# A two-layer attention and gated-MLP kernel: loads reordered, constants moved off the front of VectorE, tiles normalized one by one, and a planner with traced transfer and fetch times

## The chip, the cores and the metric

The kernel runs on one core of a Trainium2 chip. The metric is the device time of one execution in microseconds (us). Quoted times are medians of several executions.

A core has five engines that run their own instruction streams and wait for one another through semaphores: TensorE (PE, matmuls; its weight loads are PEld), VectorE (DVE), ScalarE (ACT), GpSimd (POOL) and SyncE (SP), which here only starts transfers. ScalarE starts a few transfers too, on a queue of its own.

## The reference

Two rounds of windowed attention and a gated MLP, each with a residual, on one sequence of 2048 rows of 512 elements in bfloat16.

```python
def _A_ref(x, wqkv, wo):                      # 32 heads of 16, window of 256 keys, causal
    q, k, v = split_heads(x @ wqkv)           # (cut: reshape and transpose)
    scores = einsum("bhqd,bhkd->bhqk", q, k) * Dh ** -0.5
    p = softmax(where(mask, scores, -1e9))
    return merge_heads(einsum("bhqk,bhkd->bhqd", p, v)) @ wo

def _B_ref(x, w_gate, w_up, w_down):          # F = 1792
    return (sigmoid(x @ w_gate) * (x @ w_up)) @ w_down

x = A_x
x = x + _A_ref(_layernorm(x), A_wqkv, A_wo)
x = x + _B_ref(_layernorm(x), B_w_gate, B_w_up, B_w_down)
x = x + _A_ref(_layernorm(x), A_wqkv, A_wo)   # the same weights again
x = x + _B_ref(_layernorm(x), B_w_gate, B_w_up, B_w_down)
```

## The kernel before

The rows are 16 tiles of 128, in four groups of four. The program that builds the kernel holds a **planner**: a small model of the engines and transfers that runs while the instructions are written, keeps for each engine a queue of ready tasks with a priority, and emits whatever the model finds free. On the chip each engine then executes its instructions in that fixed order. If the model is wrong about when something is ready, the order is still correct, but an engine stands behind a wait while later work would have been possible.

The assumed times of the kernel before, and the way it models a transfer and an instruction fetch:

```python
EXP_NS = 1880                 # one exponential on ScalarE
EXTRA = {"ACT": 40, "DVE": 10, "POOL": 30, "SP": 70}
COLD = 13600                  # matmuls are taken as twice as long before this time
DMA_LATENCY = 1500            # issue done to landed
FETCH = (1200, 1300)
...
    def land(self, t, since):
        if self.fetched >= since - FETCH[0]:
            self.at(self.fetched + FETCH[0] + FETCH[1], t.done.fire)
        else:
            t.done.fire()
    def dma(self, ns, nbytes, fn, deps=(), prio=5, after=0, queue="SP"):
        def go(e):
            fn()
            self.dma_free = max(self.dma_free, self.now + ns) + nbytes / 250.0
        ...
```

Each tile is normalized in three steps on two engines: its statistics on VectorE, the root (one over the square root of the variance) on GpSimd, and the normalizing itself on VectorE again. `prio` is 0 for the first group and 2 for the others; a lower number goes first, and among equals the one that was ready first.

X of tiles 8 to 11 comes behind the output weights and half of the gate and up weights:

```python
    def loads(...):
        ...                                        # (cut) x of tiles 0 to 3, two tiles at a time, on SP and ACT
        for i, k in enumerate("kqv"):              # three thirds of the qkv weights, on ACT
            self.has_wq[k] = load(self.wq[:, :, h], wq_src[:, :, h], D * D * 2, prio=0, queue="ACT" if i < 3 else "SP")
        x_group(1, 0)                              # x of tiles 4 to 7
        gap, at = 1600, 6000
        self.has_wo = load(self.wot[:], wo_src, D * D * 2, after=at)
        ...                                        # first half of gate and up, then
                x_group(2, at)                     # x of tiles 8 to 11, then the second half, down, x of 12 to 15
```

Small transfers copy v, shifted by half a tile, two tiles at a time, to Vl and Vh, for the edges of the window.

```python
        self.Vaug = [big.tile([P, NBG, VW], BF16, name=f"Vaug{i}") for i in range(3)]
        ...
            dst = self.Vaug[gi % 3][:, t % NBG, 0:VS * H]...       # the copy of tile t out of PSUM
        ...
                to, of = dst[e * HP:e * HP + HP, :, e * n:e * n + n], V[z:P:2, o:o + 2, e * n:e * n + n]
                parts.append(pl.dma(580, HP * n * 4, lambda to=to, of=of: nc.sync.dma_start(out=to, in_=of), deps, 3).done)
```

Where the model sees PE without work, it emits four dummy matmuls, so that the granted clock stays up:

```python
    def keep_warm(self, bank):
        for i in range(4):
            nc.tensor.matmul(self.banks[bank][:, 0:P], lhsT=self.ident[:], rhs=self.ident[:], start=True, stop=True)
        pl.count(4)
        pl.matmul("d", 4 * 56)
```

The softmax here doesn't subtract the row's maximum and nothing guards it: scores larger than these inputs give would overflow.

## Time and profile before

| kernel before | value |
|---|---|
| time, median of 3 (lowest to highest) | 552.1 us (551.35 to 553.03) |
| span of the profiled run | 551.2 us, granted clock 0.997 |
| PE busy, next engine | 96%, VectorE 75% |
| dummy matmuls in the order | 88 (56 of them first) |

The prediction below shows the page's shares, PE's waits, the opening and two stretches of the clock. A row of the timeline is: start, duration, engine, line, operation, result <- inputs, sizes, count; in brackets, how long the engine stood idle before it and what released it.

Two rows of the timeline of the kernel before matter later and aren't in the prediction. They show when the second group of tiles (4 to 7) got going:

```profile
23.71 0.41 DVE L520 TENSOR_SCALAR xn<-xsb,st 128x512 bf16<-128x512 bf16 x1
...
26.31 0.81 PE L572 MATMUL bank<-xnT,wq 128*128 128x512 bf16 x2
```

Its last tile, 7, is normalized at 23.71, and PE starts q of the group (512 columns at a time) at 26.31, without a wait in front of it.

### The profile page before, as it was taken

The numbers are of one execution on the slowest core, as the hardware profiler recorded it, in microseconds if no ns is written. First come the engines' busy times: TensorE is split into PE (matmuls) and PEld (weight loads), VectorE is DVE, ScalarE is ACT, GpSimd is POOL, SyncE is SP. The second block draws the span as 40 slices with busy tenths as digits, with TensorE's granted clock in tenths as the row PEclk, the third lists the DMA queues.
The fourth block names the chain that finished last, engine by engine and source line by source line (L and its number), as shares of the span: only waits on it lengthen the run. The fifth ranks groups of instructions, "written<-read, shape, count | busy, mean of one in ns | idle before, by whom it ended". The sixth has DMA issues, their size and how long they took to land.

```text
span 551.2 us, 24123 instructions
## 1 busy us (share of the span) xinstructions
PE 527.5 (96%) x10851; PEld 354.7 (64%) x10944; DVE 414.5 (75%) x906; ACT 395.5 (72%) x459; POOL 63.1 (11%) x145
## 2 busy tenths in 40 slices
PE   7998999999999999989999999999999999999996
PEld 6546857756657656656566765666656666767874
DVE  6997889788799799679677696868767677756432
ACT  3897878888888887657587877868788776742321
POOL 5221110110011120002110021000100000000000
PEclk8999999999999999999999999999999999999999
DMA  8694412322334332214401143022541332122000
GB/s 276 209 170 147 51 39 56 65 44 63 46 52 75 64 40 58 45 32 98 70 6 37 42 89 62 12 51 61 96 62 23 40 81 60 41 50 59 21 21 29
DMA packets 97015, 36.41 MB, mean 66 GB/s; under 512 B 79248, under 2 KB 96912, under 8 KB 96912
## 3 DMA queue, kind: packets, MB, share of 16 engines
q1 hardware_dynamic: 95040, 33.04, 30.1%
q8 instruction: 85, 1.39, 1.1%
q10 hardware_dynamic: 1872, 1.84, 1.1%
q14 instruction: 18, 0.15, 0.1%
HBM read 9.70 MB, written 2.10 MB: 21 GB/s over the span
## 4 chain that ended last, share of the span: by engine, by line
PE 87%; DVE 4%; DMA 4%; issue 3%; ACT 1%; POOL 0%; DVEq 0%; ACTq 0%
PE bank L662 33%; PE bank L695 16%; PE bank L932 8%; PE Sps L853 7%; PE bank L723 5%; PE bank L572 5%; PE bank L637 5%; PE bank L601 5%; PE Sps L863 2%; DMA xnT<-xn 2%; DMA OnT<-On 1%; ACT PTring L905 1%; DVE st L498 1%; PE bank L532 1%; DMA out_dram<-xsb 1%
## 5 line engine op out<-in xcount | busy, mean ns | idle before, releaser
L905 ACT ACTIVATE PTring<-Sps 128x2048 bf16<-128x2048 f32 (+1 forms) x122 | 225.9, 1851 | 55.2 <-PE Sps L853 52.3
L662 PE MATMUL bank<-xnT,wg 128*128 128x256 bf16 (+1 forms) x1064 | 140.6, 256 | 0.1
L662 PE MATMUL bank<-xnT,wu 128*128 128x256 bf16 (+1 forms) x1064 | 140.5, 256 | 0.0
L674 ACT ACTIVATE th<-bank 128x256 bf16<-128x256 f32 x224 | 80.2, 384 | 47.9 <-PE bank L662 42.4
L677 DVE SCALAR_TENSOR_TENSOR hT<-th,bank 128x256 bf16<-128x256 bf16 x224 | 87.5, 414 | 30.8 <-ACT th L674 29.8
L695 PE MATMUL bank<-wd,hT 128*128 128x512 bf16 x402 | 103.6, 379 | 2.5 <-issue 1.0
L662 PEld LDWEIGHTS <-wg 128*128 128x128 bf16 x1064 | 88.5, 98 | 23.5 <-issue 1.7
L662 PEld LDWEIGHTS <-wu 128*128 128x128 bf16 x1064 | 90.9, 98 | 12.3 <-issue 0.9
L503 POOL TENSOR_SCALAR st<-st 128x1 f32<-128x1 f32 x64 | 18.6, 291 | 442.4 <-DVE st L499 442.4
L905 ACT ACTIVATE edge<-Sps 128x2048 bf16<-128x2048 f32 (+1 forms) x32 | 56.7, 1773 | 16.8 <-PE Sps L863 16.1
L791 DVE TENSOR_TENSOR PTring<-PTring,mask 128x1024 bf16<-128x1024 bf16 x64 | 44.0, 687 | 30.8 <-ACT PTring L905 30.7
L695 PEld LDWEIGHTS <-hT 128*128 128x128 bf16 x448 | 41.8, 98 | 37.8 <-issue 0.8
L932 PE MATMUL bank<-PTring,Vaug 128*32 128x64 bf16 (+1 forms) x2880 | 52.1, 203 | 3.6 <-issue 3.5
L932 PEld LDWEIGHTS <-Vaug 128*32 128x32 bf16 x2880 | 44.0, 97 | 13.7 <-issue 10.6
L555 DVE CAST OTs<-bank 128x512 bf16<-128x512 f32 x54 | 39.2, 728 | 15.1 <-PE bank L932 14.7
L853 PE MATMUL Sps<-qT,kTp 32*128 32x64 bf16 (+3 forms) x1856 | 47.8, 218 | 1.4 <-ACT PTring L905 0.3
L853 PEld LDWEIGHTS <-kTp 32*128 32x128 bf16 x1856 | 24.5, 92 | 36.7 <-issue 35.0
L932 PE MATMUL bank<-edge,Vl 128*32 128x64 bf16 x1024 | 44.5, 193 | 0.0
L498 DVE BATCH_NORM_STATS2 st<-xsb 128x6 f32<-128x512 bf16 x64 | 43.7, 683 | 0.4
L791 DVE TENSOR_TENSOR edge<-edge,maske 128x1024 bf16<-128x1024 bf16 x60 | 40.8, 682 | 3.3 <-ACT edge L905 3.2
L504 POOL TENSOR_TENSOR st<-st,nhalf 128x1 f32<-128x1 f32 x64 | 40.9, 640 | 5.3
L932 PE MATMUL bank<-edge,Vh 128*32 128x64 bf16 x896 | 40.8, 193 | 0.0
(72 smaller groups left out, 527.1 us busy)
## 6 DMA issues: line engine op xcount, KB each, us to landing
Vl<-Vaug SPq DMA_DIRECT2D x32, 68.0 KB, 2.2
out_dram<-xsb SPq DMA_DIRECT2D x32, 64.0 KB, 1.9
Vh<-Vaug SPq DMA_DIRECT2D x28, 68.0 KB, 2.3
wg<-in_B_w_gate_dram SPq DMA_DIRECT2D x2, 896.0 KB, 11.6
wu<-in_B_w_up_dram SPq DMA_DIRECT2D x2, 896.0 KB, 9.5
wd<-in_B_w_down_dram SPq DMA_DIRECT2D x7, 256.0 KB, 4.4
wq<-in_A_wqkv_dram ACTq DMA_DIRECT2D x3, 512.0 KB, 8.0
xsb<-in_A_x_dram SPq DMA_DIRECT2D x6, 256.0 KB, 6.4
```

The lines of the kernel that those rows point to most:

```text
L498: nc.vector.bn_stats(out=st[:, 0:6], in_=self.xsb[:, t, :])
L504: nc.gpsimd.tensor_tensor(out=st[:, 8:9], in0=st[:, 9:10], in1=self.nhalf[:], op=ALU.pow)
L555: self.nc.vector.tensor_copy(out=out, in_=in_)
L572: return [(mm_ns(w), lambda kt=kt, o=o: nc.tensor.matmul(self.banks[bank][:, o:o + w], lhsT=self.wq[:, kt, cq * P:cq * P + P], rhs=self.xn ...
L662: return [(mm_ns(w), lambda i=i, j=j, fc=fc, wt=wt, kt=kt: nc.tensor.matmul(pt[:, i, j, :], lhsT=wt[:, kt, fc * P:(fc + 1) * P], rhs=self. ...
L674: nc.scalar.activation(out=box["th"][0][:], in_=pt[:, 0, :], func=AF.Tanh, scale=0.5)
L677: nc.vector.scalar_tensor_tensor(out=self.hT[:, chunk, :], in0=box["th"][0][:], scalar=1.0, in1=pt[:, 1, :], op0=ALU.add, op1=ALU.mult)
L695: nc.tensor.matmul(self.banks[bank][:], lhsT=self.hT[:, c, o:o + P], rhs=self.wd[:, fc, :], start=fc == 0, stop=fc == FC - 1)
L791: done = pl.task({"DVE": dve_bf_ns(1024)}, lambda e: nc.vector.tensor_tensor(out=r, in0=r, in1=m.to_broadcast([P, 16, HP]), op=ALU.mult), ...
L853: nc.tensor.matmul(self.sps[:, m, o:o + n * HP], lhsT=kTp[32 * m:32 * m + 32, i, tt, e, :], rhs=self.qT[32 * m:32 * m + 32, i, q0:q0 + n * ...
L905: nc.scalar.activation(out=out, in_=src, func=AF.Exp, scale=scale)
L932: nc.tensor.matmul(o, lhsT=Va[:, c0:c0 + 32], rhs=p(h), start=k == 0 or t == 0, stop=k == len(parts) - 1 or t == 0, tile_position=(0, 32 * g))
```

## The change

The intent: let VectorE reach x sooner (its memsets go to GpSimd or stay behind, the masks wait), normalize the first tiles one by one so that PE starts sooner, bring all weights in the order in which they are wanted, and let the planner work with times taken from traces: how long a transfer needs to land, when an instruction block is fetched and what that delays. The core of the diff:

```diff
-EXTRA = {"ACT": 40, "DVE": 10, "POOL": 30, "SP": 70}
+EXTRA = {"ACT": 40, "DVE": 10, "POOL": 30, "SP": 0}
-COLD = 13600
+COLD = 5200
-DMA_LATENCY = 1500
-FETCH = (1200, 1300)
+LAND = 1230
+BULK = (240.0, 370.0)
+LANES = 8
+LEAD = (65, 40)
+LINE_NS = 3550
+FETCH = (1200, 2300)
@@ a transfer lands a fixed time after its issue, later if a fetch falls into it, or behind the bulk loads
+    def land(self, t, end):
+        base, nbytes, bulk = t.transfer
+        if bulk:
+            self.dma_free = max(self.dma_free, end + 1500) + nbytes / bulk
+            at = self.dma_free
+        else:
+            at = end + base
+            for f in self.fetches[-3:]:
+                if end < f + FETCH[0] < at - 400:
+                    at = max(at, f + FETCH[1] + (1550 if f + FETCH[0] < end + 500 else 1100))
+            at = max(at, self.dma_free + 300)
@@ loads
-        for i, k in enumerate("kqv"):
-            h = slice("qkv".index(k) * D, ("qkv".index(k) + 1) * D)
-            self.has_wq[k] = load(self.wq[:, :, h], wq_src[:, :, h], D * D * 2, prio=0, queue="ACT" if i < 3 else "SP")
+        self.has_wq["q"] = self.has_wq["k"] = both([
+            load(self.wq[:, k:k + 2, 0:2 * D], wq_src[:, k:k + 2, 0:2 * D], 4 * P * D * 2, prio=0, queue=q)
+            for k, q in ((0, "ACT"), (2, "SP"))])
+        self.has_wq["v"] = load(self.wq[:, :, 2 * D:3 * D], wq_src[:, :, 2 * D:3 * D], D * D * 2, prio=0, queue="ACT")
+        x_group(1)
+        self.has_wo = load(self.wot[:], wo_src, D * D * 2)
+        x_group(2)
+        gu = [load(w[:, k:k + 2, :], src[:, k:k + 2, :], 2 * P * F * 2)
+              for w, src in ((self.wg, wg_src), (self.wu, wu_src)) for k in (0, 2)]
+        self.has_gu = both(gu)
+        at = 26000
+        x_group(3, at)
@@ constants: the memsets of Vl go to GpSimd, as 32-bit words
-            eng = nc.vector if z == 0 else nc.gpsimd
             for V in self.Vd[z]:
-                eng.memset(V[0:HP, :, n:VW], 0.0)
+                for part, a, b in ((slice(0, HP), n, VW), (slice(HP, P), 0, n), (slice(HP, P), 2 * n, VW)):
+                    nc.gpsimd.memset(V[part, :, a:b].bitcast(F32), 0.0)
@@ masks behind the first roots
-        a = pl.task({"POOL": 900}, mask, prio=7, port=True)
+        a = pl.task({"POOL": 900}, mask, [self.roots["p", 0, 0, NBG - 1]], prio=7, port=True)
@@ one by one
-        c = pl.task({"DVE": 406}, apply, [b.done], prio, can, port=True)
+        c = pl.task({"DVE": 406}, apply, [b.done], -1 if key == ("p", 0, 0) else prio, can, port=True)
@@ the transpose after attention
-        b = pl.dma(1800, 262144, turn, [box[0], box[1]], 0 if early else 2)
+        b = pl.dma(1250, 262144, turn, [box[0], box[1]], 0 if early else 2, base=1950)
```

Cut: the model of fetched instruction blocks, the limit of eight transfers in flight, helper functions, and further issue times (1210 to 1240 ns and the like). The arithmetic is unchanged.

## The prediction

> **What bounds the kernel now.** I read the page's shares first, then the list of what TensorE (PE) waited for, then the opening of the timeline, then the table of stretches.
>
> ```profile
> PE 527.5 (96%) x10851; PEld 354.7 (64%) x10944; DVE 414.5 (75%) x906; ACT 395.5 (72%) x459; POOL 63.1 (11%) x145
> ...
> PEclk8999999999999999999999999999999999999999
> ...
> q8 instruction: 85, 1.39, 1.1%
> ```
>
> PE is busy for 96% of the span and no other engine for more than 75%. The page's mean for a gate matmul, 256 ns, is its whole latency and not its share of the time, so I took the start-to-start distances of the matmuls from the trace. A 256-column gate or up matmul follows its neighbour after 109 ns, a 512-column one after 216 ns, nearly everywhere. Setting each kind of neighbour at its median distance and adding up gives 529.7 us of PE work that cannot be squeezed without dropping instructions. The span is then: start 1.44 us, work 529.7, tail after the last matmul starts 4.5, and the rest, about 15.6 us, is waiting and slow clock: PE falls 5.5 us behind those medians in the first 22 us, 2.1 more at 42.8, and 8 more after 60. That rest is all that a reordering can win.
>
> The waits of PE, in us in total, times, longest:
>
> ```profile
> PE bank L932 <- issue: 3.5, 2, 2.3
> PE bank L572 <- DMA xnT<-xn: 3.1, 2, 2.0
> PE bank L532 <- DVE xn L520: 2.0, 1, 2.0
> PE bank L1112 <- POOL ident L438: 1.4, 1, 1.4
> PE bank L723 <- DMA OnT<-On: 1.2, 2, 0.7
> ```
>
> These five make 11.2 us. The first is PE with no instruction to run, the second and fifth are DMA transposes that land late, the third is the first normalized tile. The fourth is the start itself, which the change leaves alone.
>
> The opening (start us, duration us, engine, line, work, count):
>
> ```profile
> 4.83 0.64 DVE L498 BATCH_NORM_STATS2 st<-xsb 128x6 f32<-128x512 bf16 x1
> ...
> 8.00 1.02 DVE L520 TENSOR_SCALAR xn<-xsb,st 128x512 bf16<-128x512 bf16 x3
> ...
> 8.44 1.42 PE L532 MATMUL bank<-ident,xn 128*128 128x128 bf16 x12 [1.96 <-DVE xn L520]
> ...
> 9.67 0.61 PE L601 MATMUL bank<-xnT,wq 128*128 128x128 bf16 x4
> ```
>
> VectorE (DVE) starts the statistics at 4.83 although the first part of x was in at 4.02 (ScalarE's table load is released by it then): memsets were still in front. It then takes all four tiles' statistics before the first is normalized at 8.00. The dummy warm-up matmuls ended at 6.47, so PE idles 1.96 us, and then runs slowly:
>
> ```profile
> 5.00:10.00 5.00, 3.04 (x41) 2.84 (x39) 4.81 (x18) 1.27 (x4) 3.08 (x8) 0.85 1.07 359
> 10.00:15.00 5.00, 4.95 (x69) 3.73 (x69) 2.53 (x8) 3.25 (x7) 0.42 (x2) 0.81 1.09 367
> ```
>
> Third from the end is the granted clock (0.85, 0.81), last the GB/s. Every later stretch up to 500 us has clock 1.00.
>
> **What the Trainium skill says.** "Perfetto Trace Analysis", opening note: matmul busy time is a bad measure of distance to the roofline, because matmuls are pipelined; weight-load share is a better one. The trace agrees: 96% busy beside 64% weight load, and 256 ns of latency beside 109 ns of spacing. "TensorE: Matmul & The Clock Gate", Part 1: PE runs at half clock until a window of about 3.4 us has been busy, and falls back after an idle one; warm spacing is N/2.4 ns + 2.5. The trace agrees (109 and 216 ns warm, 107 ns for 128 columns cold), and the slow stretch follows the idle gap. "Runtime: NRT & Kernel Launch", Instruction fetch mechanics: instructions stream in in blocks of 16 KiB, 256 instructions, "mostly hidden". The trace has 85 such packets (1.39 MB), and 21,890 PE instructions make 85.5 blocks; but the 2.3 us wait on "issue" follows the start of one such packet by 0.4 us, so it isn't always hidden. "DMA: Bandwidth & Descriptors", Specifications: some 358 GB/s of HBM per core; the trace shows 359 to 369 between 5 and 20 us.
>
> **The change part by part.** The kernel carries a planner that fixes the order of instructions from assumed times, so I compared the built order of both programs; arithmetic is the same.
>
> (a) Off the front of DVE: the six memsets of Vl (2 x (0.31 + 0.28 + 0.09) = 1.4 us) go to GpSimd, as 32-bit words. GpSimd's own six drop by about half (0.60, 0.55, 0.15 us now) and it gets twelve, at some 0.3, 0.28 and 0.1 us: 4 x 0.7 = 2.7 us, estimated from those rows, and its two masks (0.9 us) move behind the first roots. It stays free before the first root is wanted. DVE can take x at about 4.1 instead of 4.83: 0.7 us.
>
> (b) One by one: in the new order the first normalize stands behind three statistics, not four: 0.82 us less (0.64 + 0.18). First normalize at 4.1 + 3 x 0.82 = 6.6, first transposes at about 7.0 against 8.44. The mask preparation on DVE (1.5 us from 8.94, ahead of the fourth tile) comes after the fourth.
>
> (c) Loads: the weights of q and k come as one pair of transfers right behind the first x, on both queues. With x that is 1.5 MB; at 367 GB/s 4.1 us. Before, the k third landed at 8.2 (the x transfer that waited for its semaphore started at 8.23) with about as many bytes ahead. So I expect q and k whole at 8.0 to 8.5, and the first k matmul near 8.3 against 9.67. Output and gate/up weights come earlier, the first gate/up matmul is not bound by them (47.3 us before).
>
> (d) More warm-up: in the built order 156 dummy matmuls stand against 88. At 56 ns warm, 68 more cost 3.8 us. They stand in PE's stream, so they cost unless they lie in a wait. 64 (56 before) come first: from 1.44, with about 1.7 us lost to the cold clock, until 6.8; so they cover the gap that was idle, and the clock should not fall back. The other 92 (32) all stand among the first 1,231 of 11,012 matmuls.
>
> (e) The plan: switches between matmul layouts are 380 before, 381 after. The same medians give 534.4 us of work for the new order, 4.7 more, of which 4.0 are dummies.
>
> **The sum.** Gains: the wait for xn 2.0; slow clock and small waits up to 22 us 5.5 - 2.1 - 1.7 = 1.6, of which I take 1.0; DMA transposes 3.1 + 1.2 + 0.4 of smaller ones = 4.7, of which I give the better plan 70%, 3.3; fetch 3.5, of which 2.0: the wait before the end should go, the one at 233 us may stay, since the new order again has two short blocks together at the change of layers. Together 8.3. Costs: 4.7 by the medians. Net -3.6 on 552.1; a little more for later small waits, -4.3: **547.8 us**, 0.8% faster. Where I chose are the 70% and the 2.0.
>
> **The rivals.** First: the dummies fill waits that were there anyway, and all waits but the cold clock go. Then 552.1 - 15.6 + 1.7 + 4.7 = 542.9, 1.7% faster: even this stays within 2%. For it speaks how closely matmuls keep their medians; against it, that DMA waits move rather than vanish. Second: the new plan guesses wrong, and starves PE early: gate/up now waits for all of its weights, and the first gate/up comes 158 PE matmuls later in the order. If two waits of 2 to 3 us appear on top of the dummies, 552 to 554. For it: the planner itself inserts 92 dummies, that is, sees PE without work. Third: another engine bounds. DVE at 75% and ACT at 72% with equal work speak against it; no change.
>
> **Range and chances.** 543.5 takes almost all of the waits, 552.5 loses the whole gain. Faster by over 2% needs under 541.1, less than the first rival's floor: 4%. Slower by over 2% needs over 563, eleven us of new waits with PE still bound: 3%. Within 2%: 93%.
>
> **What would show it.** First transposes at 6.8 to 7.3 us and no wait of PE on xn over 0.5; granted clock nearer 1 in 5 to 15 us; first k matmul near 8.3; 156 dummies at 56 ns; waits on xnT and OnT together under 2 us; one issue wait of about 2 us near 230. It is wrong if PE waits on weights or x between 8 and 60 us, if waits after 100 us stay at 8 us, or if the tail differs from 4.5.

## More of the kernel before

```python
    def layer_norm(self, key, t, deps, prio):
        ...                                        # (cut)
        a = pl.task({"DVE": 910}, stats, deps, prio, lambda: self.has("st"))
        b = pl.task({"POOL": 800}, root, [a.done], prio)
        c = pl.task({"DVE": 406}, apply, [b.done], prio, can, port=True)   # can: one of three xn buffers is free
        ...                                        # tiles 0 to 7: PE transposes xn; 8 to 15: a DMA transpose

    def feed(self):
        for t in range(NBG, NT):
            g = t // NBG
            if t not in self.fed and self.slot >= self.first[0, max(0, (g - 1) * NBG - 2 - 12)] + (t % NBG) * 1 + 0 * (g == 1):
                self.fed.add(t)
                self.layer_norm(("p", 0, g), t, [self.has_x[t]], 2)
```

So tiles 4 to 15 may take their statistics as soon as their x is there.

The v projection of each group goes to one of three buffers that hold four tiles each.

## The result, and the profile after

The changed kernel took **560.39 us** (559.27 to 562.14, 4 runs), beside 552.57 us (551.35 to 555.38, 4 runs) for the kernel before on the same chip. The ratio is **1.0142**, 95% interval 1.0107 to 1.0178: 1.4% slower, and well outside the predicted range. A ratio here is the mean time of one kernel's fast runs over that of the other's of the same rounds, so it is not quite the ratio of the medians quoted. Executions over 1.5% slower than the fastest of the same kernel are left out of the means. Below, 1.0142 is always the number to compare with; the kernel before ran along in each batch.

The page of the kernel after:

```profile
PE 540.1 (97%) x11012; PEld 357.7 (64%) x11012; DVE 408.7 (73%) x888; ACT 402.2 (72%) x471; POOL 65.2 (12%) x151
...
PEclk9999999999999998999999999999999999999999
...
q8 instruction: 86, 1.41, 1.1%
```

PE shows 12.6 us more busy time, yet the two can't be set against each other: the kernel after runs 68 more dummies, and the trace of the kernel before lacks 93 matmul records (10851 beside 10944 weight loads on its page; here both are 11012). The cold first slice of the clock is gone. What PE waited for in the kernel after (xnT is the transposed normalized x, OnT the transposed output of attention):

```profile
PE bank L563 <- DVE xn L550: 2.3, 1, 2.3
PE bank L632 <- DMA xnT<-xn: 2.1, 1, 2.1
PE bank L1143 <- POOL ident L469: 1.4, 1, 1.4
PE bank L603 <- DVE hT L708: 1.4, 1, 1.4
PE bank L754 <- DMA OnT<-On: 1.2, 2, 0.6
PE bank L963 <- DVE PTring L822: 1.1, 3, 0.7
PE bank L693 <- issue: 0.8, 1, 0.8
```

The wait on instruction issue shrank from 3.5 to 0.8 us. The wait for the first normalized tile did not go. Waits on hT (the MLP's product) and on the masked exponentials (PTring) are new on the list. The seven make 10.3 us, beside 11.2 us for the five of before that the prediction shows; with all smaller entries the two lists make 13.6 and 14.6. So this list doesn't explain 7.4 us of span.

The opening of the kernel after:

```profile
3.84 0.69 DVE L528 BATCH_NORM_STATS2 st<-xsb 128x6 f32<-128x512 bf16 x1 [0.54 <-DMA xsb<-in_A_x_dram]
...
7.56 0.69 DVE L528 BATCH_NORM_STATS2 st<-xsb 128x6 f32<-128x512 bf16 x1 [2.02 <-DMA xsb<-in_A_x_dram]
...
8.39 0.70 DVE L550 TENSOR_SCALAR xn<-xsb,st 128x512 bf16<-128x512 bf16 x2
8.82 0.72 PE L563 MATMUL bank<-ident,xn 128*128 128x128 bf16 x8 [2.34 <-DVE xn L550]
...
10.05 0.39 PE L632 MATMUL bank<-xnT,wq 128*128 128x128 bf16 x4
```

VectorE is at x as soon as it lands (3.84, 0.99 us sooner than before). But the third tile's statistics wait 2.02 us for data, and the first normalize stands behind them in the order. PE starts its transposes at 8.82, not at 7.0. And yet the clock holds (third from the end is the granted clock):

```profile
5.00:10.00 5.00, 2.66 (x47) 2.39 (x45) 2.88 (x9) 0.74 (x2) 2.38 (x7) 1.00 1.04 351
10.00:15.00 5.00, 5.00 (x85) 3.76 (x83) 3.24 (x15) 3.16 (x6) 1.72 (x6) 1.00 1.09 364
```

To find where the time goes I counted **useful work**: each matmul that isn't a dummy, valued at the median start-to-start distance of its kind in the kernel before, summed in the built order and set against the start times of the trace. The lead (+) or lag (-) of a profiled run behind the kernel before, in us, at some times (my working, from the traces; redone with another way of valuing a matmul, most entries moved by less than 1 us and one by 1.8, so small differences say nothing):

| time, us | 20 | 26 | 32 | 70 | 200 | 220 | 250 | 540 |
|---|---|---|---|---|---|---|---|---|
| after | +0.3 | -0.4 | **-2.7** | **-4.3** | -2.5 | **-7.5** | -4.9 | -6.6 |

At 20 us the change has neither won nor lost, in spite of the slower front: the warm clock pays for it. 2.3 us are lost between 26 and 32, another 1.6 by 70. Around 209 a pair of waits loses 5 us; half of that comes back by 250, where the kernel before has its own 2.3 us wait on issue (at 233); 1.7 more are lost later. The stretch at 26 in the kernel after, with two rows of VectorE from before it:

```profile
16.58 0.68 DVE L528 BATCH_NORM_STATS2 st<-xsb 128x6 f32<-128x512 bf16 x1
...
24.22 0.69 DVE L528 BATCH_NORM_STATS2 st<-xsb 128x6 f32<-128x512 bf16 x1
...
27.02 0.73 DVE L550 TENSOR_SCALAR xn<-xsb,st 128x512 bf16<-128x512 bf16 x2
```

```profile
27.78 1.08 ACT L584 CAST Vaug<-bank 128x512 bf16<-128x512 f32 x2 [1.77 <-DMA Vl<-Vaug]
```

```profile
28.42 0.21 PE L963 MATMUL bank<-PTring,Vaug 128*32 128x64 bf16 x4 [0.56 <-ACT Vaug L584]
...
29.08 0.83 PE L1143 MATMUL bank<-ident 128*128 128x128 bf16 x12
30.68 0.41 PE L884 MATMUL Sps<-qT,kTp 32*128 32x128 bf16 x24 [0.77 <-ACT PTring L936]
...
31.26 2.32 PE L603 MATMUL bank<-xnT,wq 128*128 128x512 bf16 x10
```

Those three fences are rows of VectorE, ScalarE and PE. The last VectorE row is tiles 7 and 11: tile 7 is normalized at 27.02, 3.3 us later than before. ScalarE stood 1.77 us before it could copy v: the copy waits for the transfer that carries the *other* two tiles of the same buffer away. PE runs twelve dummies in a row, waits twice, and starts q of the second group at 31.26 instead of 26.31. Dummies don't show as waits, so PE's list of waits missed most of this.

VectorE's rows just before tell why tile 7 is late. In the kernel after, VectorE takes the statistics of all eight tiles 4 to 11 from 14.14 us on (the last at 25.04) and normalizes all eight by 27.75, because x of tiles 8 to 11 arrives early now and has the same priority. The order that the program builds is 4, 5, 8, 9, 6, 10, 7, 11: the statistics at 16.58 are tile 8's, and tile 7's come only at 24.22. In the kernel before VectorE does only tiles 4 to 7 in that time, and the statistics of tiles 8 to 11 start at 26.76. The extra normalized tiles also take from the three xn buffers.

### The profile page after: what moved, and what is told of

Its sections match the earlier page's. It is cut to its first block, busy times and chain, and to the rows that moved or that the text cites. A ratio compares the mean times of both kernels' runs of the same rounds, so it can differ in the third digit from the quotient of the medians.

```text
span 558.6 us, 24388 instructions
## 1 busy us (share of the span) xinstructions
PE 540.1 (97%) x11012; PEld 357.7 (64%) x11012; DVE 408.7 (73%) x888; ACT 402.2 (72%) x471; POOL 65.2 (12%) x151
## 4 chain that ended last, share of the span: by engine, by line
PE 84%; DMA 7%; DVE 5%; ACT 3%; issue 1%; SPq 0%; ACTq 0%; DVEq 0%
PE bank L693 32%; PE bank L726 17%; PE bank L963 8%; PE Sps L884 6%; PE bank L632 5%; PE bank L754 5%; PE bank L603 4%; PE bank L668 3%; DMA xnT<-xn 3%; PE Sps L894 2%; ACT PTring L936 2%; DMA Oq<-OTs 1%; DMA xsb<-in_A_x_dram 1%; DMA OnT<-On 1%; DVE st L528 1%
## 5 line engine op out<-in xcount | busy, mean ns | idle before, releaser
L726 PE MATMUL bank<-wd,hT 128*128 128x512 bf16 x448 | 114.8, 380 | 0.0
L533 POOL TENSOR_SCALAR st<-st 128x1 f32<-128x1 f32 x64 | 20.4, 318 | 447.1 <-DVE st L529 447.1
L963 PEld LDWEIGHTS <-Vaug 128*32 128x32 bf16 x2880 | 44.5, 97 | 10.7 <-issue 7.4
```

Of the source, the lines that this page charges most:

```text
L726: nc.tensor.matmul(self.banks[bank][:], lhsT=self.hT[:, c, o:o + P], rhs=self.wd[:, fc, :], start=fc == 0, stop=fc == FC - 1)
L963: nc.tensor.matmul(o, lhsT=Va[:, c0:c0 + 32], rhs=p(h), start=k == 0 or t == 0, stop=k == len(parts) - 1 or t == 0, tile_position=(0, 32 * g))
```

## The experiments

Eighteen kernels ran; all gave the right result. Theory A: the loss comes from the start, where (1) early x of tiles 8 to 11 crowds tiles 4 to 7 out of VectorE and the xn buffers, and (2) copies into a v buffer wait for a transfer that reads its other half. Rival B: the extra dummies themselves cost. Rival C: the new planner makes a worse order everywhere. Rival D: any order differs by chance, and the order of before was a tuned lucky one. In diffs, `...` stands for an unchanged part of a line.

### Are the dummies the cost?

The first run keeps only the first 64 of the 156 dummies, in the order of after:

```diff
-        for i in range(4):
+        self.warmed = getattr(self, "warmed", 0) + 1
+        for i in range(4 if self.warmed <= 16 else 0):
```

> The changed kernel in exactly its order, but of its 156 dummy matmuls only the first 64 are issued; nothing else moves. Theory that dummies cost because they stand in TensorE's stream: 92 x 56 ns = 5.2 us less, about 555. Rival, that they only fill waits that are there anyway: 559.5 to 560.5, and the waits of TensorE between 26 and 63 us grow by about 5 us in the trace.

Measured: 568.59 us, ratio 1.0274 (1.0242 to 1.0306). Slower than the changed kernel, which neither side expected. My waits-and-slow-clock count after 70 us rises from 10.0 to 16.4 us. There is a confound: 184 instructions fewer shift the blocks in which PE's instructions are fetched against the plan. So I left the instructions in and made the 92 later dummies thin:

```diff
+            w = P if self.warmed <= 16 else 16
-            nc.tensor.matmul(self.banks[bank][:, 0:P], lhsT=self.ident[:], rhs=self.ident[:], ...)
+            nc.tensor.matmul(self.banks[bank][:, 0:w], lhsT=self.ident[:], rhs=self.ident[:, 0:w], ...)
```

> The changed kernel in its order, but the 92 dummies after the first 64 are 16 columns wide and not 128. The number of instructions stays, so that the instruction blocks fall where they fell, which they did not in the run without the dummies. Theory that dummies cost in TensorE's stream: at some 25 to 30 ns less each, 2 to 3 us less, 557.5. Rival, that they lie in waits: no change, 559.5 to 560.5.

Measured: 560.82 us, ratio 1.0141 (1.0110 to 1.0172), against 1.0142. The thin ones follow one another after 25 ns and not 56, so 92 of them take 2.9 us less of PE's stream (my estimate), and none of it shows in the time. A gain of that size lies only just outside what the two intervals allow, and in the profiled run the clock was at half once more than in after (from 31.75 to 35.17 us). So rival B falls as the cause of the 1.4%; that the dummies cost nothing at all is not shown.

### One part alone, and one part undone

The two small parts, each alone on the kernel before. `consts_alone` moves the memsets and masks (the built order of PE is the same as before); `prio_alone` is the one line of "one by one".

> The kernel before, with only the memsets and the masks moved off the front of VectorE. The order of TensorE is the same as before, instruction for instruction. Theory that the front is bound by VectorE's memsets and masks: first normalized tile 0.7 us earlier, 551.5 to 552.3. Rival: the first x or the fourth tile decides, nothing moves, 552.3 to 552.9.

> The kernel before with only the one-by-one priority of the first four normalizations. Theory that the first normalized tile is on the path: 1.4 us earlier first transpose, 551 to 552. Rival: it only re-plans what follows (108 dummies and not 88), and comes out at 553 to 556.

Measured: `consts_alone` 551.59 us, ratio 0.9970 (0.9944 to 0.9997), as expected; `prio_alone` 553.56 us, 1.0011 (0.9970 to 1.0053), between its two expectations. Neither alone makes the loss. Then the two large parts: the planner alone on the kernel before, and the changed kernel with its planner or its loads put back.

> The kernel before with only the new planner (its transfer and fetch times and its cold time), old loads, old memsets, old priority. If its better times of transfers help, as the change meant: 548 to 551, with waits of TensorE after 100 us of 4 us or less against 8. If they don't: 553 to 557, waits after 100 us of 8 us or more.

> The changed kernel with the old planner (old constants, old transfer and fetch times), all other parts of the change kept. If the new planner makes the loss: back to 551 to 554. If the order of loads makes it: 558 or more, since this order has even more dummies, 188.

> The changed kernel with the old order of loads (k, q, v one by one on the scalar queue, gate and up in column halves around x tiles 8 to 11), all else of the change kept. The run with the old planner and the new loads was 1.7% slower than before. If the loads alone make the loss: 551 to 554. If the loss is in any new planning, whatever the loads: 557 or more.

| run | new loads | new planner | dummies | median us of fast runs | ratio (95%) |
|---|---|---|---|---|---|
| consts_alone | no | no | 88 | 551.59 | 0.9970 (0.9944 to 0.9997) |
| plan_alone | no | yes | 128 | 562.46 | 1.0190 (1.0150 to 1.0230) |
| undo_loads | no | yes | 132 | 564.79 | 1.0256 (1.0195 to 1.0317) |
| undo_plan | yes | no | 188 | 562.94 | 1.0168 (1.0137 to 1.0198) |
| after | yes | yes | 156 | 560.39 | 1.0142 (1.0107 to 1.0178) |

`undo_loads` and `undo_plan` keep the two small parts. The record calls `plan_alone` and `undo_loads` unclear, since their intervals cross 2%; the three fast runs of `undo_loads` lie between 563.71 and 571.08, and its trace has 5.7 us of waits on issue, beside 3.5 in the kernel before. With either large part and not the other, the loss is at least about that of both together. `undo_plan` is 10 us of useful work behind at 60 us (-9.9) and no further behind at the end (-10.1): the new loads hurt the start, and with the old planner nothing after it. So a planner cannot be all of it, and rival C in its plain form falls. In both `plan_alone` and `undo_plan` copies into a v buffer wait for the Vl transfer (2.3 and 3.8 us); in the kernel before none does. In `prio_alone` one waits too, 1.9 us, and nothing is lost: such a wait costs only where PE needs what stands behind it.

### Is the order of before a lucky one?

A five-nanosecond change of one assumed time gives another order of the kernel before:

```diff
-EXP_NS = 1880
+EXP_NS = 1885
```

> The kernel before with one assumed time of its planner nudged by 0.3% (1885 ns for an exp and not 1880): no load, buffer or operation changes, only the order from matmul 460 on. Theory that the constants before were tuned until the order came out well, so that any new order loses: 555 to 558. Rival, that the order is robust and the loss comes from the change's own parts: 551.5 to 554.

Measured: 551.44 us, ratio 0.9979 (0.9950 to 1.0009). Rival D falls, as far as one other order can tell.

### The two suspects, one at a time and together

(1) Tiles 8 to 15 take their statistics after everything else:

```diff
-                self.layer_norm(("p", 0, g), t, [self.has_x[t]], 2)
+                self.layer_norm(("p", 0, g), t, [self.has_x[t]], 2 if g == 1 else 4)
```

> The changed kernel, with one number changed: the normalization of tiles 8 to 15 gets a lower priority than before in the planner, so that tiles 4 to 7 (the next stage of scores) come first. Theory that the early load of x tiles 8 to 11 lets their normalization take VectorE and the three normalized buffers from tiles 4 to 7: the 3 us that are lost between 26 and 32 us come back, q and k of the second group start near 27 us and not 31, 556 to 557.5. Rival, that the loss lies in the new planner's later order or in the dummies: 559 to 562.

Measured: 558.36 us, ratio 1.0088 (1.0055 to 1.0121), between the two expectations. Some of the loss went, but q of the second group began at 33.00 us and not near 27: the trace shows that the second suspect grew. VectorE and then PE in this run:

```profile
25.12 0.69 DVE L586 CAST Vaug<-bank 128x512 bf16<-128x512 f32 x1 [3.62 <-DMA Vl<-Vaug]
28.12 0.69 DVE L586 CAST Vaug<-bank 128x512 bf16<-128x512 f32 x1 [2.30 <-DMA Vl<-Vaug]
28.73 0.40 DVE L550 TENSOR_SCALAR xn<-xsb,st 128x512 bf16<-128x512 bf16 x1
```

```profile
29.19 0.61 PE L563 MATMUL bank<-ident,xn 128*128 128x128 bf16 x4 [5.49 <-DVE xn L550]
```

Two v copies now stand on VectorE, 3.62 and 2.30 us, for the transfer that reads the same buffer; tile 7's normalize is behind them, and PE waits 5.49 us for it. The wait that one reads at PE ("xn from VectorE") is not VectorE's own slowness: its cause is two steps back, a transfer.

(2) The first v buffer is split in two buffers of two tiles, so that copies of tiles 2 and 3 have nothing to do with the transfer of tiles 0 and 1. The order stays exactly that of after:

```diff
-        self.Vaug = [big.tile([P, NBG, VW], BF16, name=f"Vaug{i}") for i in range(3)]
+        self.Vaug = [[big.tile([P, 2, VW], BF16, name=f"Vaug{i}{h}") for h in range(2)] if i == 0 else
+                     [big.tile([P, NBG, VW], BF16, name=f"Vaug{i}")] for i in range(3)]
```

(and four lines that pick the buffer of a tile.)

> The changed kernel in exactly its order, but the first of the three buffers of v is two buffers of two tiles each, so that the copies of v tiles 2 and 3 no longer wait for the transfer that reads tiles 0 and 1 (a wait of 1.8 us in the trace of the changed kernel, none before). Theory that this wait, which the planner doesn't know, costs startup time: the wait is gone, the waits of TensorE between 22 and 70 us fall from 3.7 to 2.5 or less, time 1 to 2 us less than the changed kernel's 560. Rival, that the copy was not on the path: 559.5 to 560.5.

Measured: 559.08 us, ratio 1.0104 (1.0084 to 1.0125), some 0.4% better than after, which is at the edge of the noise. The wait on Vl is gone from the list: so it came from one buffer holding both, not from data that was needed. At 32 us this run lags 0.2 us where after lags 2.7. But it falls back to -3.5 by 70 and -7.2 at the end: alone it only moves the loss.

Both together:

> The run with tiles 4 to 7 normalized first (558.4 us; it had a 5.5 us wait of TensorE at 29 us behind two v copies held by the same transfer), in the same order, with v's first buffer split. If both causes hold, the early normalization of x tiles 8 to 11 and the held v copies, the 5.5 us come back: 552 to 554. If that wait only moves elsewhere: 556 or more.

Measured: **552.58 us, ratio 0.9987** (0.9960 to 1.0015). The whole loss is back. Against `x2_later`, in the same order, the split is worth 1.0%, well outside the noise. VectorE (tile 7) and then PE in this run:

```profile
24.05 0.40 DVE L551 TENSOR_SCALAR xn<-xsb,st 128x512 bf16<-128x512 bf16 x1
```

```profile
26.72 0.38 PE L604 MATMUL bank<-xnT,wq 128*128 128x512 bf16 x1
```

Tile 7 is normalized at 24.05, and q of the second group starts at 26.72, as before (23.71 and 26.31). Useful work against the kernel before, with the other runs of this part:

| time, us | 20 | 26 | 32 | 70 | 200 | 220 | 250 | 540 |
|---|---|---|---|---|---|---|---|---|
| after | +0.3 | -0.4 | -2.7 | -4.3 | -2.5 | -7.5 | -4.9 | -6.6 |
| x2_later | +1.6 | -0.7 | -4.5 | -4.4 | -3.4 | -4.5 | -3.0 | -3.9 |
| split_v | +1.1 | +0.2 | -0.2 | -3.5 | -1.7 | -6.8 | -5.8 | -7.2 |
| x2_later_split | +0.5 | +0.5 | +1.0 | +2.3 | +2.7 | +1.5 | +3.0 | +2.9 |
| before_combo | -0.3 | -0.3 | +0.3 | +0.6 | +1.3 | +0.8 | +3.5 | +3.3 |

Of the 9.5 us between after and x2_later_split at the end, 6.6 are there at 70 us, in the stretch that the two mends touch. The rest, 2.9 us, comes in a part of the order that changed along with them (104 dummies stand in this order, not 156), so it is not shown to be theirs.

The split on the planner alone, where x of tiles 8 to 11 comes late as before:

> The kernel before with the new planner alone (562.5), in the same order, with v's first buffer split (its v copy waited 2.3 us). Theory: 1.5 to 2.5 us less, 560 to 561; the rest of its loss, waits after 70 us of 11.5 against 8.3 us, stays, since it is of another cause. If the held copy were the whole cause: 553 to 555.

Measured: 561.81 us, ratio 1.0159 (1.0134 to 1.0184), 1.0190 without. The v wait explains little there, if anything. Most of what the new planner costs with the old loads lies after 70 us: 13.5 us of waits and slow clock, beside 8.3 in the kernel before.

### The new planner's late waits

Adding up waits and slow clock after 70 us for each profiled run, I found 4.9 to 9.2 us (mean 7.2) in the eight runs of the old planner and 7.4 to 14.0 (mean 10.7) in eight of the new one, leaving out `no_dummies` and the padded runs below. Its purpose was to lessen them. A candidate cause: it assumes that a transfer lands at the traced median (1230 ns after the issue; 1500 before), without margin. `after_pad` adds 400 ns of margin, `after_pad8` 800, and `x2_later_split_pad` 400 to the order with both mends:

```diff
-LAND = 1230
+LAND = 1630
...
-        b = pl.dma(1250, ..., base=1950)
+        b = pl.dma(1250, ..., base=2350)
```

(and 1520 to 1920 for the v transfers.)

> The changed kernel with 400 ns added to each of the three landing times that the new planner assumes (1230, 1950 and 1520 ns). Theory that the planner leaves no margin: waits of TensorE after 70 us fall from 10.0 us to 7 or less; the start keeps its loss; 1.008 to 1.012 times before. Rival, that late waits of an order are a matter of luck within some 3 us: 8 to 13 us after 70 us and 1.011 to 1.019.

> The changed kernel with 800 ns of margin instead of 400. If margin is the cause, waits after 70 us stay at 7 us or less and the ratio at 1.006 to 1.011. If it was luck, they go back to 9 to 12 us and the ratio to 1.011 to 1.018.

> The changed kernel with both mends of the start and 400 ns of margin in the assumed landing times. If the margin is worth some 3 us after 70 us whatever the order, waits there fall from 7.4 to 4 to 6 us and the ratio from 0.9987 to 0.993 to 0.997. If the gain of the margin in the changed kernel was luck of that order, they stay at 7 to 11 us and the ratio at 0.997 to 1.004.

| run | margin ns | waits after 70 us | median us | ratio (95%) |
|---|---|---|---|---|
| after | 0 | 10.0 | 560.39 | 1.0142 (1.0107 to 1.0178) |
| after_pad | 400 | 6.7 | 557.29 | 1.0082 (1.0052 to 1.0112) |
| after_pad8 | 800 | 6.8 | 556.34 | 1.0041 (1.0004 to 1.0078) |
| x2_later_split | 0 | 7.4 | 552.58 | 0.9987 (0.9960 to 1.0015) |
| x2_later_split_pad | 400 | 7.8 | 554.15 | 0.9994 (0.9961 to 1.0027) |

With margin the late waits of the changed kernel fell by 3.3 and 3.2 us, and the ratio of `after_pad8` fell below its expectation. (The ratios of `after_pad8` and `x2_later_split_pad` flatter: the kernel before had a median of 554.98 in their batch, 552.4 in that of `after_pad`.) But margin also makes another order, with 164 dummies and not 156, and in the mended kernel it took nothing, a miss. So margin helped one kernel, by itself or by its order, and is not shown to be a general cause; why the new planner's orders wait longer late **stays open**.

### Towards a faster kernel

The old planner with the new loads and both mends:

> Old planner with the new loads, constants and priority, and both mends (statistics of tiles 8 to 15 late, first v buffer split). If the two causes at the start hold whatever the planner, the 1.0168 of the old planner with the new loads falls to 0.996 to 1.002. If the new planner is needed for the new loads, it stays above 1.008.

Measured: 555.52 us, ratio 1.0056 (1.0016 to 1.0097), between the two expectations. The mends worked: the run lags 2.6 us at 20 and 3.5 at 60, where `undo_plan` lags 9.9. What is left happened at the front. There the statistics of the third tile waited for x until 8.15, PE waited 3.6 us for the first normalized tile, and the granted clock was 0.50 to 0.52 between 8 and 14 us.

That made me look at the third tile's statistics in every trace. They start between 5.99 and 7.16 us in the nine runs with the old loads (in four of them without a wait for x), and between 5.74 and 8.15 in the eleven with the new ones, always after such a wait; the means are 6.4 and 7.1. The late half of that pair is the one on SP's queue: its last row ended at 7.04 us in the kernel after and at 5.01 in the kernel before. In the kernel after, from 4.5 to 6.0 us, ScalarE's queue moved 355 KB, most of it q and k weights in rows of 2 KB, while SP's queue, most of it x in rows of 1 KB, moved 80 KB. It is tempting to blame the longer rows. But in the kernel before, with rows of 1 KB on both queues, the same stretch gave 435 KB to ScalarE's queue and 47 KB to SP's. What makes the landing vary, from kernel to kernel and from run to run, was not tested.

Last, the kernel before with the good small parts: constants moved, one by one, and the split; loads and planner as before. Beside it the same without one by one:

> The kernel before with the memsets and masks moved, tiles normalized one by one, and the first v buffer split; loads and planner as before. The sum of consts_alone (0.997), prio_alone (1.001, which had a 1.9 us v wait that the split removes) gives 0.994 to 1.000.

> The kernel before with memsets and masks moved and the first v buffer split, otherwise in the order of before. Before had no wait on that buffer, so the split should give nothing beyond consts_alone: 0.995 to 0.999. If the buffer also cost something unseen in before, under 0.994.

Measured: `before_combo` **548.97 us, ratio 0.9934** (0.9904 to 0.9964), the fastest kernel, just under its expectation, and about 2% faster than the changed one (0.9934 over 1.0142, from different batches); `before_consts_split` 552.65 us, 1.0005 (0.9981 to 1.0029), slightly over its expectation. PE's waits in `before_combo`:

```profile
PE bank L533 <- DVE xn L520: 1.7, 3, 0.8
PE bank L1115 <- POOL ident L439: 1.4, 1, 1.4
PE bank L725 <- DMA OnT<-On: 1.2, 1, 1.2
```

The 3.5 us wait on issue of the kernel before is not among them, only short ones of up to 0.4 us. Useful work agrees: within 1.3 us of level until 44 us, +0.6 at 70, +0.8 at 220, +3.5 at 250. So most of this gain isn't the earlier front; it is an order in which the fetch of instructions happens not to hold PE up. `before_consts_split`, without that luck, has 3.5 us of it and no gain. I would not call the 0.7% a property of its parts.

## Why the prediction was wrong

**The step that failed** is the sum: it set gains of 8.3 us against 4.7 us of dummies, for 4.3 us less in the end, and only the second rival had a term for a starved PE. In the runs the dummies cost nothing that could be seen; the wait for the first normalized tile grew by 0.3 us instead of losing 2.0, the DMA waits lost 1.0 us instead of 3.3, and 4.3 us of useful work were lost by 70 us, where early x of tiles 8 to 11 and a shared v buffer kept tiles 4 to 7 from PE.

**What held.** PE stayed the bound, 97% busy with no other engine over 73%. VectorE began at 3.84 (4.1 predicted). The issue wait shrank by 2.7 us, where I gave it 2.0; but it is 5.7 us in `undo_loads`, so its size comes with the order and is no merit of the plan. The class, within 2%, was right too.

**What came true by luck.** The clock stayed at 1.00 from 5 to 15 us, but not because the 64 warm-up dummies covered the gap, as step (d) said. They ended at 6.48, as the 56 had (6.47), since the clock rose sooner, at 4.20 and not at 5.11; then PE stood idle for 2.34 us, longer than the 1.96 of before. In every trace the clock changes only at whole multiples of 3.41 us after its first change (in the kernel before at 5.11, 8.52 and 11.94). The gap of before lies within one such step, and the clock was at half in the next; the gap of after is cut in two at 7.61 (4.20 + 3.41), with 1.1 and 1.2 us on its sides, and the clock held. Where the steps fall differs between the traces. That fits here and is no full rule: in `prio_alone` PE was busy for 1.46 us of the step from 232.40, beside 1.45 of the step from 5.11 in the kernel before, and there the clock held.

**Step (b), first transposes at 7.0.** I let the three statistics run back to back from 4.1. The third waited for x until 7.56; first transposes came at 8.82, and the 2.0 us wait for xn became 2.3. I had read the landing of the first pair from the profile and not asked for the second, beside which the new weight transfers now run; why it came late stays open (see below). Where that pair did land early (5.91, in `split_v`), transposes began at 7.18, so the sum was right and its input was not.

**Step (c), first k matmul near 8.3.** It came at 10.05, for the same reason. Its list of waits has none on the q and k weights.

**Step (d), the dummies cost 3.8 us.** No cost of theirs was seen (1.0141 with thin ones, 1.0142 with full ones). They were a symptom: the planner emits them where it sees PE without work. Had I read 92 dummies as some 5 us that the planner itself expects PE to starve (92 x 56 ns, my estimate), I would have looked for the starved stretch in the built order.

**The sum, 70% of the DMA waits.** Waits on xnT and OnT were 4.3 us before (3.1 + 1.2) and 3.3 after, not under 2. And waits on hT and PTring, 2.5 us together, came in. In my count, waits and slow clock after 70 us rose from 8.3 to 10.0. The prediction named waits that stay at 8 us (after 100 us) as a sign of being wrong, and it is what came.

**What was missing.** The second rival saw an early starvation from a plan that guesses wrong, and gave 552 to 554 us. The kind was right; the place was not (q of tiles 4 to 7, not gate and up) and the size was too small. The list of loads showed that x of tiles 8 to 11 moves ahead of all gate and up weights. I followed that to its arrival, and not to what an early arrival *releases*: four more statistics and normalizes in VectorE's order, ahead of work that PE waits for. `x2_later_split` shows it, together with the v buffer, where copies waited for a transfer that doesn't touch their tiles. Both mends together bring 1.55% (1.0142 to 0.9987), one alone 0.5% and 0.4%, the latter at the edge of the noise: with the first alone the v copies held PE up instead (5.49 us), with the second alone the lead was lost again by 70 us.

**What stays open.** Why the new planner's orders wait longer after 70 us, of which margin may explain some in one kernel; and why the second x pair is there anywhere between 5.74 and 8.15 us with the new loads. Rival D was tested on the kernel before alone: no run gives the changed kernel another order for no reason, so what of the 0.5% of `x2_later`, which is another order too, is mere order isn't known. The split keeps the order, and the early part of the gain can be read in the traces.

## What to carry to other kernels

When a load is moved forward, ask not only what it delays but what its early arrival lets start: tasks of equal priority then take the engine and the buffers from those on the critical path. Count useful work over time when waits don't explain a loss, because filler instructions hide starvation inside busy time; a rise in the filler of a planned order is a warning, not a price. And try mends together as well as alone: each here was worth half a per cent or less, and both 1.5.

## What the Trainium skill lacked or had wrong

- "DMA: Bandwidth & Descriptors", Queues, rings and completion order, says that an engine takes turns between queues packet by packet, but not what share of the bytes two busy queues then get. From 4.5 to 6.0 us ScalarE's queue moved 355 KB and SP's 80 KB in the kernel after (rows of mostly 2 KB and 1 KB), and 435 KB and 47 KB in the kernel before (1 KB on both). SP's queue may have had too little left to move in part of that time; this was not taken apart.
- "TensorE: Matmul & The Clock Gate", Part 1, ties the fall to half clock to an idle window of about 3.4 us; of short idles it tells only in one example, and gives no share that is enough. In the kernel after, waits of 0.68 us (before 209.72) and 2.13 us (before 212.61) with short matmuls between were enough: PE was busy for 1.32 of the 2 us from 208, 0.48 of the 2 from 210 and 0.39 of the 1 from 212, and the granted clock was 0.50 from 213 to 215. So here PE did not stand still for a whole window.
- "Runtime: NRT & Kernel Launch", Instruction fetch mechanics, gives no cost for a fetch that isn't hidden: in the kernel before, PE's wait on issue was 3.5 us in two pieces, the longer 2.3.
